# An attention-plus-gated-FFN kernel: fp32 k loads on SyncE's queue, block 1's q and k ahead of the last weights, crossbar transposes issued a phase sooner

## The chip, the cores and the metric

The kernel runs on one core of one Trainium2 chip. The metric is the device time of one execution in microseconds (us), lower is better. Profiled spans are some 2 us shorter than the times (250.0 against 251.96 us for the same execution before the change), so spans are compared with spans and times with times. TensorE is called PE in the profile, VectorE DVE, ScalarE ACT, GpSimd POOL, SyncE SP; PEld is the loading of weights into PE, which overlaps PE. "SPq" and "POOLq" are the sequencers of those engines, which issue DMAs.

## The reference, cut to what matters

q, k and v are fp32 of shape (4 batches, 8 heads, 768 positions, 64). A decayed linear attention runs over them; its output, as 3072 tokens of 512 features, goes through a gated feed-forward layer.

```
kv_state = 0
for each block of positions:
    intra = ((q k^T) * decay mask) v
    inter = (q * lam^(i+1)) kv_state
    out   = intra + inter
    kv_state = lam^block * kv_state + (k * lam^(block-1-i))^T v

y = (sigmoid(x Wg) * (x Wv)) Wo        # 512 -> 1536 -> 512
```

The kernel works in bf16 and in blocks of 128 positions, six of them (0 to 5). For one block and all four batches it needs q and k with the head dimension on the partitions, which is a transpose.

## The kernel before: the parts that the change touches

One program order is written for all engines, and each engine executes its own instructions in that order. What an engine has to wait for is decided by its own queue and by data.

The loads are GpSimd DMAs, which cast fp32 to bf16 on the way. Blocks 0 and 1 are transposed on TensorE (`t_q`, `t_k`, results tq and tk in PSUM). Blocks 2 to 5 are transposed by the DMA crossbar, issued by SyncE, from SBUF to SBUF (results qt and kt in the profile):

```
def xbar(n):                                     # blocks 2..5
    for c, d in (("q", QT), ("k", KT)):
        d[n] = qtp.tile([128, B, HP, C], BF16, tag=c + "t", name=c + "t")
        nc.sync.dma_start_transpose(out=d[n]..., in_=T_[c, n]...)

def e_q(n, bp):                                  # QS = transposed q times a table of lam powers, on VectorE
    src = tqs[n, bp] if n < FIRST_XBAR else QT[n][:, 2 * bp:2 * bp + 2]
    t = trsb.tile([128, 2, HP, C], BF16, tag="QS", name="QS")
    nc.vector.tensor_tensor(out=t, in0=src, in1=lamq..., op=ALU.mult)

def make_kd(n):                                  # kd = k times decay, on GpSimd
    nc.gpsimd.tensor_tensor(out=KD[n], in0=T_["k", n], in1=kds..., op=ALU.mult)
```

KS is the transposed k: ScalarE's copy of tk, or kt itself. The attention of a block is `piece_s` (scores sp = KS^T QS on TensorE), `piece_m` (MT = sp times mask, on VectorE), `piece_a` (op = MT v plus QS times state), `piece_x` (XT, the copy of op), and `piece_c` (state: cp on TensorE, sd on GpSimd, Sb on VectorE). The feed-forward is `piece_gv` (gp and vp, four matmuls each, 12 slices ft to a block; ScalarE makes sg, VectorE makes ht) and `piece_po` (po, 12 matmuls per batch, then an output store from SyncE). The attention of the next block is woven between the slices of the current one.

The head, before the first gp:

```
load(0, "q", 0, 2); ...; load(0, "k", 0, 2); ...; load(0, "q", 2, 4); ...; load(0, "k", 2, 4); load v; load weights
zeros(6)                       # filler matmuls, zps in the profile
t_q(0, 0); e_q(0, 0); zeros(2); t_k(0, 0); e_k(0, 0, parts=2); make_mask(); zeros(2)
piece_s(0, [0]); piece_m(0, 0); zeros(1); piece_s(0, [1]); piece_m(0, 1); zeros(2)
t_q(0, 1); e_q(0, 1); zeros(3); t_k(0, 1); e_k(0, 1, parts=2); ...; piece_s and piece_m of batches 2, 3; zeros(3)
for b in range(B): piece_a(0, [b]); piece_x(0, [b]); zeros(2 if b < B - 1 else 3)
```

And where the crossbar transposes stand:

```
for ft in range(4):  gv(1, ft, ...)
for tt in range(B):  po(0, tt, *[lambda: xbar(2)] if tt == 1 else loads if tt == 2 else [])   # behind two output stores
gv(1, 4, e_q(2)); gv(1, 5); gv(1, 6, piece_s(2), ...); ...
# later blocks: xbar(n+1) in the first slice of block n, behind the stores of block n-1
```

## Time and profile before

| | before |
|---|---|
| time, median of 4 runs | 252.57 us (252.32 to 255.6) |
| profiled span | 250.0 us |
| TensorE busy | 226.7 us (91%) |
| first gp (end of the head) | 20.47 us |
| first gp of block 1 | 50.19 us |
| first po of block 1 | 97.02 us |

The busy row of the page of the kernel before, and its row of the granted TensorE clock (tenths of full speed in 40 slices of 6.25 us):

```profile
PE 226.7 (91%) x1514; PEld 112.2 (45%) x1514; DVE 108.9 (44%) x181; ACT 76.2 (30%) x134; POOL 83.7 (33%) x73
...
PEclk9799999999996599999999999999999999999999
```

TensorE is nearly always busy, so what matters is where it is not. The list of its waits, kernel before (us in total, times, longest):

```profile
PE sp L207 <- DMA kt<-kb: 9.8, 1, 9.8
...
PE tq L166 <- DMA qb<-in_q_dram: 1.9, 1, 1.9
PE sp L207 <- DVE QS L179: 1.8, 1, 1.8
PE op L221 <- DVE MT L215: 1.2, 1, 1.2
```

One wait stands out, and it is for the transposed k of block 2. SyncE's own timeline before (start us, duration us, what) shows why it comes late:

```profile
61.40 2.92 SPq L293 DMA_DIRECT2D out_dram<-ob  x2
64.36 6.25 SPq L195 DMA_TRANSPOSE qt<-qb  x1
70.66 5.74 SPq L195 DMA_TRANSPOSE kt<-kb  x1
76.45 32.08 SPq L293 DMA_DIRECT2D out_dram<-ob  x6
```

The two transposes stand behind two output stores, and these wait for results of the po block. The records of the loads say that q of block 2 had landed at 55.4 us and k at 59.0. Each transpose keeps SyncE for about 6 us, and kt lands 12.84 us after its issue, at 83.5 us.

The wait costs more than itself. Busy time by stretch, before (stretch, length, then PE, PEld, DVE, ACT, POOL, granted clock, DMA share, GB/s), and the instructions behind the wait:

```profile
0.00:20.47 20.47, 14.93 (x127) 6.74 (x128) 9.93 (x16) 8.26 (x18) 17.14 (x24) 0.92 1.68 132
20.47:50.19 29.72, 27.19 (x225) 14.76 (x225) 18.72 (x32) 10.07 (x16) 25.80 (x24) 1.00 1.74 175
...
73.70:83.55 9.85, 0.00 (x1) 0.01 (x2) 1.89 (x3) 0.00 (x0) 6.05 (x4) 0.65 2.12 160
83.55:87.60 4.05, 4.05 (x25) 1.95 (x26) 1.29 (x2) 0.60 (x1) 1.15 (x1) 0.58 2.25 183
```

```profile
83.55 1.04 PE L207 MATMUL sp<-QS,kt 64*128 64x128 bf16 x16 [9.85 <-DMA kt<-kb]
...
84.52 1.89 PE L270 MATMUL gp<-XT,WG 128*128 128x512 bf16 x4
```

In the third stretch TensorE does nothing. In the fourth it works at a granted clock of 0.58, and the sixteen sp and four gp take 1.04 and 1.89 us instead of 0.62 and 1.03 elsewhere. The Trainium skill, "TensorE: Matmul & The Clock Gate", Part 1, says that TensorE's clock falls to half after an idle window and returns after a busy one; this trace agrees: TensorE stood idle from 73.70 us, and its clock is recorded at half from 76.73 to 86.97 us.

For the head, VectorE's timeline before:

```profile
7.44 0.69 DVE L179 TENSOR_TENSOR QS<-tq,lamq 128x1024 bf16<-128x1024 bf16 x1 [5.29 <-PE tq L166]
8.05 1.21 DVE L151 TENSOR_TENSOR mask<-tri,pk 128x1024 f32<-128x1024 f32 x1
11.34 2.48 DVE L215 TENSOR_TENSOR MT<-sp,mask 128x512 bf16<-128x512 f32 x4 [2.07 <-PE sp L207]
```

### The profile page before, as it was taken

Reading aid. Unit: us, or ns where it says so; the run is one execution under the profiler, and the core shown is the slowest. Engines: PE = TensorE matmul, PEld = TensorE weight load, DVE = VectorE, ACT = ScalarE, POOL = GpSimd, SP = SyncE. Lnnn points to the kernel's source line nnn. Section 1 sums busy time; section 2 is a strip of 40 time slices with the busy share of each in tenths; the row PEclk is TensorE's granted clock in tenths of the full one; section 3 lists DMA queues with packets and bytes.
Section 4 is the critical chain, followed back from the end, with each engine's and each line's share of the span. In section 5 each row is a group of like instructions: output and inputs, shape, how many; then the busy total and the mean of one; then the engine's idle time right before and its main releaser. Section 6 shows DMA issues by size and latency. Waiting matters only on the chain.

```text
span 250.0 us, 3742 instructions
## 1 busy us (share of the span) xinstructions
PE 226.7 (91%) x1514; PEld 112.2 (45%) x1514; DVE 108.9 (44%) x181; ACT 76.2 (30%) x134; POOL 83.7 (33%) x73
## 2 busy tenths in 40 slices
PE   4799999699970699999799999999999999999994
PEld 1344555454430345454345454455454464444443
DVE  1483657763013283048981058760087820143400
ACT  5152334221230024223224223324333252333211
POOL 8969958954993500029800023000000000000000
PEclk9799999999996599999999999999999999999999
DMA  8999999999999990275990273001290002200022
GB/s 52 150 175 184 159 161 174 206 159 152 184 166 136 198 109 3 84 166 93 156 91 3 90 173 73 4 0 42 87 210 0 3 0 85 87 0 0 0 87 84
DMA packets 104545, 24.89 MB, mean 100 GB/s; under 512 B 95696, under 2 KB 101584, under 8 KB 104528
## 3 DMA queue, kind: packets, MB, share of 16 engines
q0 software_dynamic: 84144, 14.16, 81.4%
q1 hardware_dynamic: 20384, 10.49, 17.8%
q8 instruction: 12, 0.20, 0.3%
q14 instruction: 5, 0.04, 0.1%
HBM read 28.32 MB, written 6.29 MB: 138 GB/s over the span
## 4 chain that ended last, share of the span: by engine, by line
PE 82%; DMA 8%; DVE 4%; SPq 3%; issue 1%; ACT 1%; POOL 1%; POOLq 0%; DVEq 0%
PE gp L270 24%; PE po L287 23%; PE vp L276 23%; DMA kt<-kb 5%; PE sp L207 3%; SPq L195 2%; PE op L227 2%; DMA kb<-in_k_dram 2%; PE zps L301 2%; PE cp L245 2%; DVE MT L215 2%; PE op L221 2%; DVE QS L179 2%; PE tk L173 1%; DVE ht L279 1%
## 5 line engine op out<-in xcount | busy, mean ns | idle before, releaser
L279 DVE TENSOR_TENSOR ht<-sg,vp 128x512 bf16<-128x512 bf16 x72 | 49.2, 686 | 105.4 <-PE vp L276 105.0
L270 PE MATMUL gp<-XT,WG 128*128 128x512 bf16 x288 | 74.9, 383 | 1.1 <-DVE XT L237 0.9
L276 PE MATMUL vp<-XT,WV 128*128 128x512 bf16 x288 | 74.3, 380 | 0.0
L273 ACT ACTIVATE sg<-gp 128x512 bf16<-128x512 f32 x72 | 43.0, 597 | 100.2 <-PE gp L270 99.1
L287 PE MATMUL po<-WO,ht 128*128 128x512 bf16 (+1 forms) x300 | 63.2, 371 | 0.0
L276 PEld LDWEIGHTS <-WV 128*128 128x128 bf16 x288 | 28.4, 99 | 34.5 <-issue 1.1
L287 PEld LDWEIGHTS <-ht 128*128 128x128 bf16 x300 | 29.1, 98 | 32.4
L270 PEld LDWEIGHTS <-WG 128*128 128x128 bf16 x288 | 26.9, 98 | 31.6 <-issue 1.3
L215 DVE TENSOR_TENSOR MT<-sp,mask 128x512 bf16<-128x512 f32 x48 | 30.5, 681 | 8.1 <-PE sp L207 8.1
L250 POOL TENSOR_TENSOR sd<-Sb,dec 128x512 f32<-128x512 bf16 x16 | 16.2, 1038 | 51.1 <-DVE Sb L258 51.1
L292 ACT COPY ob<-po 128x512 f32<-128x512 f32 (+1 forms) x24 | 13.8, 576 | 45.8 <-PE po L287 45.8
L93 POOL TENSOR_TENSOR kd<-kb,kds 128x2048 bf16<-128x2048 bf16 x5 | 18.2, 3639 | 0.0
L207 PE MATMUL sp<-QS,kt 64*128 64x128 bf16 x128 | 5.4, 228 | 11.7 <-DMA kt<-kb 9.8
L76 POOL DMA_DIRECT2D vb<-in_v_dram x8 | 11.4, 1425 | 7.3 <-issue 5.7
L258 DVE TENSOR_TENSOR Sb<-cp,sd 64x256 bf16<-64x256 f32 x32 | 13.5, 420 | 0.8
L239 ACT CAST XT<-op 128x512 bf16<-128x512 f32 x20 | 10.5, 598 | 10.1 <-PE op L227 10.1
L76 POOL DMA_DIRECT2D qb<-in_q_dram x8 | 11.8, 1478 | 3.9 <-issue 3.1
L301 PE MATMUL zps<-Sb 128*128 128x512 bf16 x30 | 10.5, 456 | 2.1 <-DVE Sb L110 2.1
L76 POOL DMA_DIRECT2D kb<-in_k_dram x8 | 11.5, 1433 | 1.8 <-issue 1.8
L179 DVE TENSOR_TENSOR QS<-qt,lamq 128x1024 bf16<-128x1024 bf16 x8 | 8.1, 1014 | 6.2 <-DMA qt<-qb 6.2
L207 PEld LDWEIGHTS <-kt 64*128 64x128 bf16 x128 | 3.9, 99 | 15.2 <-DMA kt<-kb 10.3
L188 ACT COPY KS<-tk 128x512 bf16<-128x512 bf16 (+1 forms) x6 | 4.2, 730 | 10.5 <-PE tk L173 10.5
(40 smaller groups left out, 84.8 us busy)
## 6 DMA issues: line engine op xcount, KB each, us to landing
out_dram<-ob SPq DMA_DIRECT2D x23, 256.0 KB, 2.0
qb<-in_q_dram POOLq DMA_DIRECT2D x4, 512.0 KB, 12.0
kb<-in_k_dram POOLq DMA_DIRECT2D x4, 512.0 KB, 15.1
vb<-in_v_dram POOLq DMA_DIRECT2D x4, 512.0 KB, 15.0
WO<-in_moe_w_out_dram POOLq DMA_DIRECT2D x3, 512.0 KB, 10.4
qb<-in_q_dram POOLq DMA_DIRECT2D x4, 256.0 KB, 7.6
kb<-in_k_dram POOLq DMA_DIRECT2D x4, 256.0 KB, 8.2
vb<-in_v_dram POOLq DMA_DIRECT2D x4, 256.0 KB, 8.4
```

The lines of the kernel that those rows point to most:

```text
L76: nc.gpsimd.dma_start(out=T_[c, n][:, b0:b1], in_=src[b0:b1, :, sl, :].rearrange("b h s d -> s (b h) d"))
L93: nc.gpsimd.tensor_tensor(out=KD[n], in0=T_["k", n], in1=kds.unsqueeze(1).unsqueeze(3).to_broadcast([128, B, H, D]), op=ALU.mult)
L207: nc.tensor.matmul(sp[u][:, hp, :], lhsT=KS[n, b][us, hp, :], rhs=QS[n, b][us, hp, :], start=(hp == 0), stop=(hp == HP - 1), skip_group_ch ...
L215: nc.vector.tensor_tensor(out=MT[n, b][:, u], in0=SP[n, b][u], in1=mask[:, u], op=ALU.mult)
L250: nc.gpsimd.tensor_tensor(out=sd, in0=Sb[:, b], in1=dec.unsqueeze(2).to_broadcast([128, HP, 128]), op=ALU.mult)
L270: nc.tensor.matmul(gp, lhsT=WG[:, mt, fs], rhs=x[:, mt, :], start=(mt == 0), stop=(mt == NMT - 1))
L273: nc.scalar.activation(sg, gp, AF.Sigmoid)
L276: nc.tensor.matmul(vp, lhsT=WV[:, mt, fs], rhs=x[:, mt, :], start=(mt == 0), stop=(mt == NMT - 1))
L279: nc.vector.tensor_mul(HT[n, ft], sg, vp)
L287: nc.tensor.matmul(po[:, :c1 - c0], lhsT=HT[n, ft][:, tt * 128:(tt + 1) * 128], rhs=WO[:, ft, c0:c1], start=(ft == 0), stop=(ft == NFT - 1))
L292: nc.scalar.copy(ob[:, c0:c1], po[:, :c1 - c0])
L301: nc.tensor.matmul(zps, lhsT=Sb[:, 0, 0, :], rhs=Sb[:, 0], start=True, stop=True)
```

## The change

Its intent has three parts (with them go smaller edits: 4 buffers instead of 5 for q and k, fewer and larger loads of block 1's v and of the output weights, and block 3's loads issued one po sooner):

- Head: k of batches 0 and 1 of block 0 comes as fp32 by SyncE's queue at once and is cast on VectorE, so half a k load leaves GpSimd's queue. The head works batch by batch, and there are fewer fillers (5 instead of 9 around op).
- Block 1: its k and q are loaded ahead of the last weight slices, and its TensorE transposes and scores are issued one slice sooner.
- Crossbar: block 2's transposes are issued ahead of the po block's stores, and those of blocks 3 to 5 late in the block before, ahead of its stores.

The diff, cut to its core:

```
+    T_["k", 0] = qkv.tile([128, B, H, D], BF16, tag="kb", name="kb", bufs=4)
+    load_hw("k", 0, nc.sync)                     # fp32 [128, H, D] by SyncE's queue
+    load_hw("k", 1, nc.sync)
+    nc.scalar.dma_start(out=lam_bc, in_=lam.partition_broadcast(128))
     load(0, "q", 0, 2)
-    nc.sync.dma_start(out=lam_bc, in_=lam.partition_broadcast(128))
...
-    load(0, "k", 0, 2)
...
     zeros(6)
-    t_q(0, 0)                                    # ... the head shown above
+    for b in range(2):
+        cast_hw("k", b)                          # VectorE, fp32 to bf16
+        t_("k", 0, [b]);  e_k(0, [b])
+        t_("q", 0, [b]);  e_q(0, [b])
+        if b == 0:
+            make_mask()
+        zeros(2)
+    for b in range(2):
+        piece_s(0, [b]);  piece_m(0, b);  zeros(1)
+    ...                                          # batches 2, 3; then op with 5 fillers
...
-    load_gv(8, 10); load q, k of block 1; load_gv(10, 11); load_gv(11, 12)
+    load k, q (batches 0, 1); load_gv(8, 9); load k, q (batches 2, 3); load_gv(9, 10); load_gv(10, 12)
...
-    behind[8] = [trans(1, 0)]                    # transposes of block 1
-    behind[9] = [pair(piece_s, 1, 0), m_(1, 0), m_(1, 1), trans(1, 1)]
-    behind[10] = [pair(piece_s, 1, 1), m_(1, 2)]
-    behind[11] = [m_(1, 3), att(1)]
+    behind[7] = [trans(1, 0)]
+    behind[8] = [pair(piece_s, 1, 0), m_(1, 0), m_(1, 1), trans(1, 1)]
+    behind[9] = [pair(piece_s, 1, 1), m_(1, 2), m_(1, 3)]
+    behind[11] = [att(1)]
...
-                gv(1, ft, *more[ft][:1] if ft < 2 else [])
+                gv(1, ft, *more[ft][:1] if ft < 2 else [lambda: xbar(2)] if ft == 3 else [])
-                po(0, tt, *[lambda: xbar(2)] if tt == 1 else loads if tt == 2 else [])
+                po(0, tt, *loads if tt == 1 else [])
-            gv(1, 10, *more[8])
+            gv(1, 10, *more[8], lambda: xbar(3))
-                more[0].append(lambda nx=nx: xbar(nx))
+                more[8].append(lambda nx=nx: xbar(nx + 1))
```

More of the change, by code (lines that the diff above doesn't have):

```diff
@@ L43 @@
     qkv = ctx.enter_context(tc.tile_pool(name="qkv", bufs=5))
+    hwp = ctx.enter_context(tc.tile_pool(name="hwp", bufs=4))
     qtp = ctx.enter_context(tc.tile_pool(name="qtp", bufs=2))
@@ L73, in load @@
             if (c, n) not in T_:
-                T_[c, n] = qkv.tile([128, B, H, D], BF16, tag=c + "b", name=c + "b")
+                T_[c, n] = qkv.tile([128, B, H, D], BF16, tag=c + "b", name=c + "b",
+                                      bufs=5 if c == "v" else 4)
             src = {"q": q, "k": k, "v": v}[c]
@@ L104, with load_hw @@
     lam_bc = const.tile([128, H], FP32, tag="lam_bc")
+    H32 = {}
+    def load_hw(c, b, eng):
+        src = {"q": q, "k": k}[c]
+        H32[c, b] = hwp.tile([128, H, D], FP32, tag="h32", name="h32")
+        eng.dma_start(out=H32[c, b], in_=src[b, :, 0:C, :].rearrange("h s d -> s h d"))
+    T_["k", 0] = qkv.tile([128, B, H, D], BF16, tag="kb", name="kb", bufs=4)
+    load_hw("k", 0, nc.sync)
+    load_hw("k", 1, nc.sync)
+    nc.scalar.dma_start(out=lam_bc, in_=lam.partition_broadcast(128))
     load(0, "q", 0, 2)
-    nc.sync.dma_start(out=lam_bc, in_=lam.partition_broadcast(128))
     nc.scalar.preload_act_table_set("natural_log_exp_and_others")
@@ L112 @@
     make_identity(nc, ident, nomemset=True)
-    load(0, "k", 0, 2)
     nc.gpsimd.iota(ip1, pattern=[[1, C]], base=1, channel_multiplier=0,
                    allow_small_or_imprecise_dtypes=True)
+    load(0, "k", 2, 4)
     for i, base in enumerate((-1, C - 1)):
@@ L118 @@
                        allow_small_or_imprecise_dtypes=True)
-    load(0, "q", 2, 4)
     nc.gpsimd.affine_select(out=tri, in_=tri, compare_op=ALU.is_gt, fill=1.0, base=0,
                             pattern=[[-1, C]], channel_multiplier=1)
-    load(0, "k", 2, 4)
+    load(0, "q", 2, 4)
     load(0, "v", 0, 2)
@@ L160, with t_, e_q, e_k @@
     tqs, tks = {}, {}
-    def t_q(n, bp):
-        tq = ps_at.tile([128, 2, HP, C], BF16, name="tq", tag="ps")
-        for i in range(2):
+    def t_(c, n, bs):
+        ps = ps_at.tile([128, len(bs), HP, C], BF16, name="t" + c, tag="ps")
+        for i, b in enumerate(bs):
             for hp in range(HP):
-                nc.tensor.transpose(tq[:, i, hp, :], T_["q", n][:, 2 * bp + i, 2 * hp:2 * hp + 2, :], ident)
-        tqs[n, bp] = tq
-    def t_k(n, bp):
-        tk = ps_at.tile([128, 2, HP, C], BF16, name="tk", tag="ps")
-        for i in range(2):
-            for hp in range(HP):
-                nc.tensor.transpose(tk[:, i, hp, :], T_["k", n][:, 2 * bp + i, 2 * hp:2 * hp + 2, :], ident)
-        tks[n, bp] = tk
-    def e_q(n, bp):
-        src = tqs[n, bp] if n < FIRST_XBAR else QT[n][:, 2 * bp:2 * bp + 2]
-        t = trsb.tile([128, 2, HP, C], BF16, tag="QS", name="QS")
-        nc.vector.tensor_tensor(out=t, in0=src,
-                                in1=lamq.unsqueeze(1).to_broadcast([128, 2, HP, C]), op=ALU.mult)
-        for i in range(2):
-            QS[n, 2 * bp + i] = t[:, i]
-    def e_k(n, bp, parts=1):
+                nc.tensor.transpose(ps[:, i, hp, :], T_[c, n][:, b, 2 * hp:2 * hp + 2, :], ident)
+        (tqs if c == "q" else tks)[n, bs[0]] = ps
+    def e_q(n, bs):
+        w = len(bs)
+        src = tqs[n, bs[0]] if n < FIRST_XBAR else QT[n][:, bs[0]:bs[0] + w]
+        t = trsb.tile([128, 2, HP, C], BF16, tag="QS", name="QS")
+        nc.vector.tensor_tensor(out=t[:, :w], in0=src,
+                                in1=lamq.unsqueeze(1).to_broadcast([128, w, HP, C]), op=ALU.mult)
+        for i in range(w):
+            QS[n, bs[i]] = t[:, i]
+    def e_k(n, bs, parts=1):
         t = trsb.tile([128, 2, HP, C], BF16, tag="KS", name="KS")
-        w = 2 // parts
+        w = len(bs) // parts
         for i in range(parts):
-            nc.scalar.copy(t[:, i * w:(i + 1) * w], tks[n, bp][:, i * w:(i + 1) * w])
-        for i in range(2):
-            KS[n, 2 * bp + i] = t[:, i]
+            nc.scalar.copy(t[:, i * w:(i + 1) * w], tks[n, bs[0]][:, i * w:(i + 1) * w])
+        for i in range(len(bs)):
+            KS[n, bs[i]] = t[:, i]
+    def cast_hw(c, b):
+        nc.vector.tensor_copy(T_[c, 0][:, b], H32[c, b])
     def xbar(n):
@@ L303 @@
     zeros(6)
-    t_q(0, 0)
-    e_q(0, 0)
-    zeros(2)
-    t_k(0, 0)
-    e_k(0, 0, parts=2)
-    make_mask()
-    zeros(2)
-    piece_s(0, [0])
-    piece_m(0, 0)
-    zeros(1)
-    piece_s(0, [1])
-    piece_m(0, 1)
-    zeros(2)
-    t_q(0, 1)
-    e_q(0, 1)
-    zeros(3)
-    t_k(0, 1)
-    e_k(0, 1, parts=2)
+    for b in range(2):
+        cast_hw("k", b)
+        t_("k", 0, [b])
+        e_k(0, [b])
+        t_("q", 0, [b])
+        e_q(0, [b])
+        if b == 0:
+            make_mask()
+        zeros(2)
+    for b in range(2):
+        piece_s(0, [b])
+        piece_m(0, b)
+        zeros(1)
+    t_("k", 0, [2, 3])
+    e_k(0, [2, 3], parts=2)
+    zeros(1)
+    t_("q", 0, [2, 3])
+    e_q(0, [2, 3])
     tables_late()
     zeros(2)
-    piece_s(0, [2])
-    piece_m(0, 2)
-    piece_s(0, [3])
-    piece_m(0, 3)
-    zeros(3)
+    for b in range(2, 4):
+        piece_s(0, [b])
+        piece_m(0, b)
     for b in range(B):
@@ L331 @@
         piece_x(0, [b])
-        zeros(2 if b < B - 1 else 3)
+        if b:
+            zeros(1)
+    zeros(2)
     make_kd(0)
     load_gv(6, 8)
-    load_gv(8, 10)
+    load(1, "k", 0, 2)
     load(1, "q", 0, 2)
-    load(1, "k", 0, 2)
+    load_gv(8, 9)
+    load(1, "k", 2, 4)
     load(1, "q", 2, 4)
-    load(1, "k", 2, 4)
-    load_gv(10, 11)
-    load_gv(11, 12)
-    load(1, "v", 0, 2)
-    load(1, "v", 2, 4)
-    for i in range(3):
-        load_wo(4 * i, 4 * i + 4)
+    load_gv(9, 10)
+    load_gv(10, 12)
+    load(1, "v")
+    load_wo(0, 6)
+    load_wo(6, 12)
     load(2, "qk")
@@ L373, in go @@
         def go():
-            t_q(n, bp)
-            e_q(n, bp)
-            t_k(n, bp)
-            e_k(n, bp)
+            bs = [2 * bp, 2 * bp + 1]
+            t_("k", n, bs)
+            e_k(n, bs)
+            t_("q", n, bs)
+            e_q(n, bs)
         return go
@@ L401 @@
             more[1] = [pair(piece_c, n, 1)]
-            more[3] = [lambda nx=nx: e_q(nx, 0)]
+            more[3] = [lambda nx=nx: e_q(nx, [0, 1])]
             more[4] = [pair(piece_s, nx, 0), m_(nx, 0)]
-            more[5] = [m_(nx, 1), lambda nx=nx: e_q(nx, 1)]
+            more[5] = [m_(nx, 1), lambda nx=nx: e_q(nx, [2, 3])]
             more[7] = [pair(piece_s, nx, 1), m_(nx, 2)]
@@ L424 @@
             if nx < NSTEP:
-                more[0].append(lambda nx=nx: xbar(nx))
                 more[2] += loads
+            if nx + 1 < NSTEP:
+                more[8].append(lambda nx=nx: xbar(nx + 1))
             for ft in range(NFT):
```

## The prediction

> What bounds the kernel now. The page's busy rows give TensorE 226.7 of 250.0 us: it is bound by TensorE plus a few waits. The list of waits on TensorE has one large entry: block 2's score matmuls wait 9.8 us for the crossbar transpose that makes kt. In the timeline, the transposes stand on SyncE behind two output stores that need results of the po block: qt is issued at 64.4 us, kt at 70.7, kt lands at 83.5, though their sources landed at 55.4 (q) and 59.0 (k). The stretch table shows a granted clock of 0.58 just after; 16 sp, 4 gp and 4 vp take 1.04, 1.82, 1.21 us there instead of 0.62, 0.97, 0.86: another 1.6 us. (The Trainium skill, "TensorE: Matmul & The Clock Gate", Part 1, says that an idle window halves the clock; this trace agrees.) So this place costs about 11.4 us. The first gp stands at 20.47 us. From there to 50.19 (first gp of block 1) TensorE is busy 27.2 of 29.7 us.
>
> What the change does.
> 1. Crossbar, block 2: the transposes stand ahead of the stores and wait only for their loads. SyncE takes 6 us to issue each and 12.8 us to land it while the software queue is full (later ones, on a quiet queue: 2 and 4.7). The loads land about 2 us sooner, because half a k load (1.8 us) left that queue: q about 53, k about 56.5. Estimate: qt issued 53, lands 66; kt issued 59, lands 72. TensorE will want kt at about 71.5. The wait shrinks from 9.8 to 0 to 2 us, and the slow clock goes: gain about 10.5 us. The skill ("DMA: Bandwidth & Descriptors", Issuing engines are not separate DMA queues) says that all queues share 16 engines, so I keep 12.8. Sooner issue for blocks 3 to 5 gains nothing: those landings (4.7 us) already precede their use; the 1.8 us wait at 124.8 is for QS on VectorE, 3.3 us long beside GpSimd's kd, and stays.
> 2. Head: k of batches 0, 1 lands by about 4.5 and 6 us instead of 8.8, but q (6.7, now sharing the engines: about 7.3) takes over. VectorE gets two casts (estimate 0.4 us each) and must do QS, mask (1.21), cast, QS before MT, so MT starts near 11.7 instead of 11.3. Fewer fillers around op (5 instead of 9) give 1 us back. First gp near 19.5: gain 1 us (0 to 2).
> 3. Block 1: transposes one slice sooner, so all MT are done before op; the waits op on MT (1.2) and tk on MT (0.3) go; the wait on XT (0.9) stays. Reordered weight slices should land some 3 us before use. Gain 1.4 us.
>
> Nothing after 130 us changes.
>
> Predicted: 252.5 - 10.5 - 1 - 1.4, about 240 us; 8 in 10 within 237 to 244.5. Chances: faster by over 2% 0.96, within 2% 0.03, slower 0.01.
>
> Signs: qt of block 2 issued near 53 us, kt landed near 72; TensorE's wait on kt under 2 us; no granted clock under 0.9 after 25 us; first gp near 19.5; first gp of block 1 near 47.7; the wait op on MT gone.
>
> What would make it wrong: transposes slowed further by the loads, kt landing at 75 us or later (each us costs one); q late in the head, or too few fillers, so that the first gp runs at half clock; a weight slice or v of block 1 late, stalling gp or op.

## The result, and the profile after

| | before | after |
|---|---|---|
| time, median | 252.57 us (4 runs, 252.32 to 255.6) | 240.02 us (4 runs, 239.52 to 241.19) |
| profiled span | 250.0 us | 237.8 us |
| head: start to first gp | 20.47 | 21.32 |
| block 0: first gp to first gp of block 1 | 29.72 | 28.35 |
| block 1: from there to its first po | 46.83 | 35.53 |
| the rest | 152.98 | 152.59 |

The ratio of the fast runs is 0.9484, 95% interval 0.9403 to 0.9565. A run counts as fast unless it is over 1.5% above the fastest of its kernel. All ratios here are the mean time of one kernel's fast runs over that of the other's fast runs of the same rounds, so they are not quite the ratio of the medians quoted.

The busy and clock rows of the page after:

```profile
PE 222.0 (93%) x1479; PEld 111.5 (47%) x1504; DVE 111.6 (47%) x184; ACT 76.5 (32%) x134; POOL 82.0 (34%) x70
...
PEclk9769999999999999999999999999999999999999
```

The dip in the 13th and 14th slice of the row (75 to 87.5 us) is gone; the early one, in the head, has grown by a slice. The waits of TensorE after:

```profile
PE tk L177 <- DVE kb L198: 2.9, 2, 1.6
PE sp L215 <- DVE QS L184: 2.2, 2, 1.8
...
PE tq L177 <- DMA qb<-in_q_dram: 1.6, 1, 1.6
```

There is no wait on kt any more, nor the 1.2 us of op on MT before block 1; that on QS in block 3 stayed. The waits in the head are on kb (the casts), which is new, and on q, which was 1.9 us before. SyncE's timeline after:

```profile
54.43 5.37 SPq L203 DMA_TRANSPOSE qt<-qb  x1
59.84 6.43 SPq L203 DMA_TRANSPOSE kt<-kb  x1
66.32 2.67 SPq L301 DMA_DIRECT2D out_dram<-ob  x4
```

The order is turned round: transposes first, issued as soon as q has landed (54.4 us) and, for kt, as SyncE is free; kt lands at 72.2 us. TensorE comes for it 0.9 us later and does not wait (timeline after, at full clock):

```profile
73.12 0.62 PE L215 MATMUL sp<-QS,kt 64*128 64x128 bf16 x16
...
73.67 1.04 PE L278 MATMUL gp<-XT,WG 128*128 128x512 bf16 x4
```

The head went the other way. VectorE's timeline after, and the chain of waits over the head (start, length, what):

```profile
8.65 0.42 DVE L184 TENSOR_TENSOR QS<-tq,lamq 128x512 bf16<-128x512 bf16 x1 [2.54 <-PE tq L177]
9.00 1.22 DVE L162 TENSOR_TENSOR mask<-tri,pk 128x1024 f32<-128x1024 f32 x1
10.13 0.53 DVE L198 CAST kb<-h 128x512 bf16<-128x512 f32 x1
...
13.18 2.48 DVE L223 TENSOR_TENSOR MT<-sp,mask 128x512 bf16<-128x512 f32 x4 [0.96 <-PE sp L215]
```

```profile
1.26 6.83 DMA qb<-in_q_dram
...
10.71 0.61 PE tk L177 x4
11.32 0.43 PE tq L177 x4
11.75 0.85 PE zps L309 x2
12.60 0.58 PE sp L215 x8
```

q lands at 8.1 us instead of 6.7, the mask and the second cast stand behind the QS that waits for it, and the matmuls of that stretch run at half clock. MT starts 1.84 us later than before. The stretch table after gives the head a granted clock of 0.84, against 0.92 before:

```profile
0.00:21.32 21.32, 13.49 (x115) 6.87 (x118) 11.50 (x19) 8.36 (x18) 17.27 (x24) 0.84 2.07 152
21.32:49.67 28.35, 26.75 (x221) 14.73 (x225) 18.72 (x32) 10.26 (x16) 26.00 (x23) 1.00 1.78 177
```

So in the spans of these two profiles: head +0.85, block 0 -1.37, block 1 -11.30, rest -0.39; together -12.2 us.

### The profile page after: what moved, and what is told of

It is laid out like the page before. It is cut to its first block, busy times and chain, and to the rows that moved or that the text cites. A ratio compares the mean times of both kernels' runs of the same rounds, so it can differ in the third digit from the quotient of the medians.

```text
span 237.8 us, 3703 instructions
## 1 busy us (share of the span) xinstructions
PE 222.0 (93%) x1479; PEld 111.5 (47%) x1504; DVE 111.6 (47%) x184; ACT 76.5 (32%) x134; POOL 82.0 (34%) x70
## 4 chain that ended last, share of the span: by engine, by line
PE 86%; DVE 8%; DMA 3%; issue 2%; DVEq 0%; POOLq 0%
PE po L295 26%; PE gp L278 25%; PE vp L284 25%; DVE MT L223 4%; DMA qb<-in_q_dram 3%; PE sp L215 3%; DVE QS L184 2%; PE op L235 2%; PE op L229 2%; PE cp L253 2%; DVE XT L245 1%; PE tq L177 1%; DVE mask L162 1%; PE tk L177 0%; PE zps L309 0%
## 5 line engine op out<-in xcount | busy, mean ns | idle before, releaser
L278 PE MATMUL gp<-XT,WG 128*128 128x512 bf16 x277 | 72.8, 379 | 1.7 <-DVE XT L245 1.1
L284 PE MATMUL vp<-XT,WV 128*128 128x512 bf16 x282 | 73.4, 379 | 0.4
L258 POOL TENSOR_TENSOR sd<-Sb,dec 128x512 f32<-128x512 bf16 x16 | 16.7, 1068 | 32.6 <-DVE Sb L266 32.6
L78 POOL DMA_DIRECT2D vb<-in_v_dram x7 | 10.8, 1541 | 8.0 <-issue 3.8
L247 ACT CAST XT<-op 128x512 bf16<-128x512 f32 x20 | 10.5, 597 | 8.0 <-PE op L235 8.0
L78 POOL DMA_DIRECT2D kb<-in_k_dram x7 | 10.3, 1469 | 7.5 <-issue 7.5
L309 PE MATMUL zps<-Sb 128*128 128x512 bf16 x18 | 7.6, 526 | 2.1 <-DVE Sb L122 2.1
L184 DVE TENSOR_TENSOR QS<-qt,lamq 128x1024 bf16<-128x1024 bf16 x8 | 9.3, 1159 | 0.0
L235 PE MATMUL op<-MT,vb 128*64 128x128 bf16 x192 | 7.3, 221 | 0.7 <-DVE MT L223 0.7
L84 POOL DMA_DIRECT2D WG<-in_moe_w_gate_dram x8 | 6.4, 794 | 1.1 <-DMA vb<-in_v_dram 1.1
```

The source lines that it names most:

```text
L78: nc.gpsimd.dma_start(out=T_[c, n][:, b0:b1], in_=src[b0:b1, :, sl, :].rearrange("b h s d -> s (b h) d"))
L184: nc.vector.tensor_tensor(out=t[:, :w], in0=src, in1=lamq.unsqueeze(1).to_broadcast([128, w, HP, C]), op=ALU.mult)
L258: nc.gpsimd.tensor_tensor(out=sd, in0=Sb[:, b], in1=dec.unsqueeze(2).to_broadcast([128, HP, 128]), op=ALU.mult)
L278: nc.tensor.matmul(gp, lhsT=WG[:, mt, fs], rhs=x[:, mt, :], start=(mt == 0), stop=(mt == NMT - 1))
L284: nc.tensor.matmul(vp, lhsT=WV[:, mt, fs], rhs=x[:, mt, :], start=(mt == 0), stop=(mt == NMT - 1))
```

## The experiments

Twelve kernels ran, each timed in 5 rounds against the kernel before. All gave correct results. The runs that put back parts of the kernel before are written in the changed kernel's functions; in the trace of x_only the 1514 matmuls and ScalarE's instructions stand in the same order as in that of the kernel before.

The table splits each profiled span at the same three marks as above; "MT" is the start of the first MT.

| run | time, median us | ratio to before | MT | head | block 0 | block 1 | rest | span |
|---|---|---|---|---|---|---|---|---|
| before | 252.57 | 1 | 11.34 | 20.47 | 29.72 | 46.83 | 152.98 | 250.00 |
| after | 240.02 | 0.9484 | 13.18 | 21.32 | 28.35 | 35.53 | 152.59 | 237.79 |
| x_only | 242.02 | 0.9608 | 11.69 | 22.23 | 29.71 | 35.31 | 152.96 | 240.21 |
| head_only | 252.54 | 1.0032 | 13.18 | 21.22 | 29.31 | 46.64 | 152.81 | 249.98 |
| b1_only | 252.49 | 1.0011 | 11.46 | 21.79 | 28.36 | 46.07 | 152.96 | 249.18 |
| old_head | 240.43 | 0.9545 | 11.42 | 21.48 | 28.36 | 35.30 | 152.97 | 238.11 |
| after_again | 240.27 | 0.9549 | 13.27 | 21.52 | 28.36 | 35.31 | 152.79 | 237.98 |
| mask_early | 240.14 | 0.9554 | 11.45 | 18.95 | 28.36 | 36.77 | 153.22 | 237.30 |
| k_by_pool | 242.33 | 0.9616 | 12.54 | 19.91 | 28.36 | 37.43 | 154.64 | 240.34 |
| hold_loads | 244.52 | 0.9697 | 13.18 | 21.36 | 28.36 | 37.50 | 155.30 | 242.52 |
| late345 | 239.97 | 0.9517 | 13.25 | 21.57 | 28.36 | 35.30 | 152.81 | 238.04 |
| eq_early | 241.94 | 0.9561 | 13.26 | 21.99 | 28.36 | 36.98 | 153.08 | 240.41 |
| mask_hold1 | 237.66 | 0.9425 | 11.45 | 19.10 | 28.36 | 35.31 | 154.49 | 237.26 |
| best | 235.22 | 0.9314 | 11.25 | 18.63 | 28.37 | 35.30 | 150.92 | 233.22 |

The time of one and the same kernel spreads by 0.7 to 3.7 us over its fast runs (head_only: 250.78 to 254.45), and the intervals of the ratios reach 0.4 to 0.8% to either side. Effects of about 1 us are therefore read in the stretches of the traces.

### The three parts alone

**x_only**: the kernel before with the crossbar moves alone.

```
-  po(0, tt, *[xbar(2)] if tt == 1 else loads if tt == 2 else [])
+  gv(1, 3, xbar(2)); po(0, tt, *loads if tt == 1 else [])       # and blocks 3..5 as in the change
```

> The kernel before with nothing changed but the place of the crossbar transposes. If the gain of block 2 is the transposes leaving the stores behind, kt lands near 73 us, TensorE's wait on kt falls from 9.8 us to 1 us or less, and the time is about 241.5 us. Rival: the gain also needs the k load off the software queue; then kt lands at 75 us or later, the wait stays at 2 us or more, and the time is 243 us or more.

kt landed at 74.6 us and TensorE, at 75.4, did not wait for it. Timeline of x_only:

```profile
61.85 6.98 SPq L200 DMA_TRANSPOSE kt<-kb  x1
...
75.39 0.62 PE L212 MATMUL sp<-QS,kt 64*128 64x128 bf16 x16
```

The time is 242.02 us, ratio 0.9608 (0.9553 to 0.9663). The place of the transposes alone takes 11.5 us out of block 1 (46.83 to 35.31), as much as in the full change; the k load off the software queue is not needed for that. Nor did block 3's loads, which this edit moves too, start sooner (56.9 us, before 55.8). The time lies 1.6 us above that of old_head (240.43), which has block 1's part besides; 1.36 us of it is block 0.

**head_only**: the kernel before with the new head.

> The kernel before with the new head alone (k of two batches as fp32 by SyncE's queue, new order of work, fewer fillers). Theory: the head costs time; first gp near 21.3 us instead of 20.5, and the time is about 253.4 us. Rival: loads that land 1 us sooner shorten the wait on kt, or the wait absorbs the late start; then the time is 252.6 us or less.

First gp at 21.22 us as expected, but the time did not move: ratio 1.0032 (0.9959 to 1.0105). Neither theory is told apart by the time. Its wait on kt was 9.78 us, as before.

**b1_only**: the kernel before with block 1's loads and transposes alone.

> The kernel before with block 1's order of loads and of transposes alone. Theory: first gp of block 1 near 48.8 us, and since the transposes of block 2 wait for the stores, they move sooner too: time about 251.2 us. Rival: kt's landing is set by traffic on the DMA engines, so the wait on kt grows by what block 1 saves: 252.5 us.

Block 0 took 28.36 us, 1.36 less than before, in this and in every other kernel with this part; the mechanism is there to the tenth. By time the run is inconclusive: 252.49 us, ratio 1.0011 (0.9953 to 1.0069). In its profile the head, which is that of before, took 21.79 instead of 20.47 us and gave block 0's gain away. The time does show it in the pair x_only and old_head, which differ by this part alone: 1.6 us.

**old_head**: the changed kernel with the head of before.

> The changed kernel with the head of before. Theory A: the head costs its 0.85 us to the end, so without it the first gp stands at 20.5 us and the time is 239.2 us. Theory B: without it q and k of block 2 land about 1 us later, kt lands near 73.2 us and TensorE, which comes 0.85 us sooner, waits about 1 us for it: the time stays at 240.0 us.

240.43 us, and no wait on kt (it landed at 72.8 us, TensorE came at 73.3). Both theories assumed a first gp at 20.5 us; it came at 21.48. So the head of before is not fixed: four profiles with it gave 20.47, 22.23, 21.79 and 21.48 us, mean 21.5. The six profiles with the new head gave 21.32, 21.22, 21.52, 21.36, 21.57 and 21.99, mean 21.5. The records of the granted clock differ in these heads: in the one of 20.47 us a single half-clock stretch of 3.4 us after the first full-clock one, in that of 22.23 us one of 6.8 us. The record starts only at its first event (14.6 us in b1_only, 14.0 us in old_head); that the clock was at half until then is read from the fillers, 0.60 to 0.63 us each there and 0.38 us later. The skill ("TensorE: Matmul & The Clock Gate", Part 1) says that the window by which the clock is set runs freely and isn't started by the kernel; these runs fit it. My reading of the two first profiles, that the head costs 0.85 us, fell: on the mean of these profiles it costs and gains nothing, though the old head's four scatter by 1.8 us, so that a few tenths can't be excluded. Inside the head two things cancel: the first MT starts 1.7 us later (mean 13.2 against 11.5), and from there to the first gp it is 1.7 us less (8.3 against 10.0).

### Where the head's gain went, and what stands behind it

**after_again**: the changed kernel once more, as a control.

> The changed kernel once more, as the control of this call: about 240.0 us, first gp near 21.3 us or within 1 us of it[...].

240.27 us, first gp at 21.52.

**mask_early**: casts and mask ahead of the first QS on VectorE.

```
     for b in range(2):
         cast_hw("k", b);  t_("k", 0, [b]);  e_k(0, [b])
+    make_mask()
+    for b in range(2):
         t_("q", 0, [b]);  e_q(0, [b])
-        if b == 0: make_mask()
         zeros(2)
```

> The changed kernel with both casts and the mask on VectorE ahead of the first q scaling, which waits for q until 8.1 us. Theory: the head is lost on VectorE's order (mask and second cast behind the late q); MT then starts near 10.2 us instead of 13.2, first gp near 18.5 instead of 21.3. kt still lands near 72.2 us, so TensorE, wanting it at 70.4, waits 1.8 us and the time is about 239.0 us. Rival: the half clock and the landing of the loads set the head; then MT starts within 1 us of before and the time is 240.0 us.

MT starts at 11.45 us, 1.8 sooner than in the control, and the first gp comes 2.6 us sooner (18.95). VectorE's order was the larger part of what the new head lost. The 0.8 us behind MT go with a half clock that ended at 12.4 us instead of 15.8. Of the expected 3.0 us for MT, 1.2 did not come; the two sets of zps and the second tq still run slowly here, which is the likely reason. The time is that of the control, 240.14 us (238.67 to 242.08). In the profile 1.9 of the 2.6 us are given back: 1.5 in block 1, 0.4 in the rest, where the wait on QS is 2.2 instead of 1.8 us. The waits of TensorE in mask_early:

```profile
PE sp L215 <- DVE QS L184: 2.2, 1, 2.2
...
PE sp L215 <- DMA kt<-kb: 1.4, 1, 1.4
```

kt lands at 72.2 us (71.9 in the control), and TensorE, which now comes at 70.8, waits 1.4 us for it. That wait is back as soon as the head is faster. It hides another: QS of block 2, 3.59 us long beside GpSimd's sd, ends at 71.7 us.

**k_by_pool**: k of batches 0 and 1 by GpSimd's queue again, no casts, the rest as changed.

```
-    load_hw("k", 0, nc.sync);  load_hw("k", 1, nc.sync)
+    load(0, "k", 0, 2)                           # GpSimd, behind q
-        cast_hw("k", b)
```

> The changed kernel with k of batches 0 and 1 loaded by GpSimd's queue with the cast in the DMA, as before the change, no casts on VectorE, all else as changed. Theory: the fp32 loads delay q from 6.7 to 8.1 us; here q lands near 6.6 and k near 8.9, MT starts near 12.3 us instead of 13.2, and loads of block 2 land about 1 us later. Time 239.5 to 240.5 us: the fp32 loads buy nothing by themselves. Rival: they buy time in the head, and the time rises to 241 us or more.

q landed at 6.1 us and k at 8.6; MT started at 12.54, 0.7 us sooner than in the control, and the first gp stood at 19.91, 1.6 us sooner. So the fp32 loads with their casts cost the head time: they delay q from 6.1 to 8.1 us. What lies behind MT, 0.9 of the 1.6 us, goes with a half clock that ended at 12.0 us instead of 15.8 and isn't shown to be theirs. (The skill, "DMA: Bandwidth & Descriptors", Issuing engines are not separate DMA queues, says that all queues run on the same 16 engines; the q load, 4.8 us without the two fp32 loads (k_by_pool) and 6.8 us beside them, agrees.) My expected time was wrong, though: 242.33 us. In block 2 VectorE's QS ran beside GpSimd's kd and sd for 4.65 us and TensorE waited 2.05 us for it, longer than kt would have held it (72.6 us landing against 71.8). In block 3, behind the wait on QS, this run had 3.4 us of half clock. So the time rises as the rival said, but not for its reason.

**hold_loads**: kd of every block ahead of the next block's loads on GpSimd.

```
-    loads = [load(nx + 1, "qkv"), make_kd(nx)]
+    loads = [make_kd(nx), load(nx + 1, "qkv")]
```

> The changed kernel with kd issued ahead of the next block's loads on GpSimd, so that block 3's loads start near 62 us instead of 54.8, after k of block 2 has landed. Theory: these loads are what slows the transposes of block 2 (12.4 us from issue to landing); kt then lands before 69 us instead of 72.2. No wait on kt is left to save, so the time stays at 240.0 us, unless kd leaves the QS that waits 1.8 us, which would give 238.5. Rival: v of block 2 alone is enough to slow them, and kt lands at 71 us or later.

The DMA list of hold_loads, over the stretch with block 2's transposes (last number: us from issue to landing):

```profile
qt<-qb SPq DMA_TRANSPOSE x1, 10.5
kt<-kb SPq DMA_TRANSPOSE x1, 9.2
```

In the control the two took 12.0 and 12.1 us. kt landed at 68.5 us: the loads of block 3 are what slows it, as the theory had it. But the time rose to 244.52 us. kd of blocks 3 and 4 now ran at the moment of a QS, which took 3.6 us (77.5) and 3.5 us (106.3) instead of 0.7; TensorE waited 2.1 and 2.6 us for them, and behind the second its clock was at half for 3.4 us. I had not expected these.

**late345**: transposes of blocks 3 to 5 back to their later place.

> The changed kernel with the transposes of blocks 3, 4 and 5 put back to their later place behind the stores; that of block 2 stays early. If their earlier issue gains nothing, as predicted, the time is 240.2 us, within 0.5 of the control, and no wait on kt shows. Rival: the earlier issue takes a wait away there; then a wait on kt or qt of 0.5 us or more shows in a later block and the time is 241 us or more.

239.97 us and no wait on kt: the earlier issue of those three blocks gains nothing, as predicted.

### VectorE's QS beside GpSimd

In the changed kernel, at the wait in block 3 (timeline after, lines of GpSimd, VectorE and TensorE):

```profile
108.46 3.65 POOL L95 TENSOR_TENSOR kd<-kb,kds 128x2048 bf16<-128x2048 bf16 x1
109.33 3.33 DVE L184 TENSOR_TENSOR QS<-qt,lamq 128x1024 bf16<-128x1024 bf16 x1
...
112.72 0.62 PE L215 MATMUL sp<-QS,kt 64*128 64x128 bf16 x16 [1.84 <-DVE QS L184]
```

QS starts 0.9 us after kd, ends 0.6 us after it, and takes 3.33 us; all QS of the same size with nothing beside them take 0.68 or 0.69. The skill, "SBUF — State Buffer", Who interferes with whom, says that VectorE and GpSimd share one pair of SBUF ports as an exclusive lock, and that a VectorE instruction with two SBUF inputs contends with a GpSimd instruction that reads SBUF; this agrees. The traces hold the counterpart: QS of block 1 has the same size but reads tq from PSUM, and wholly inside a kd it takes 0.68 us. Timeline of x_only:

```profile
43.25 3.66 POOL L94 TENSOR_TENSOR kd<-kb,kds 128x2048 bf16<-128x2048 bf16 x1
44.55 0.68 DVE L181 TENSOR_TENSOR QS<-tq,lamq 128x1024 bf16<-128x1024 bf16 x1
```

**eq_early**: the second QS of a block straight behind the first.

```
-    more[3] = [e_q(nx, [0, 1])];  more[5] = [m_(nx, 1), e_q(nx, [2, 3])]
+    more[3] = [e_q(nx, [0, 1]), e_q(nx, [2, 3])];  more[5] = [m_(nx, 1)]
```

> The changed kernel with the second q scaling of a block issued straight behind the first on VectorE, two weight slices sooner. Theory: the wait of 1.84 us on QS in block 3 comes from VectorE's QS and GpSimd's kd running at the same time, 3.3 us instead of 0.7; here QS runs while GpSimd only issues loads, takes 0.7 us, the wait is gone, and the time is 238.4 us. Rival: QS is slow for another reason (its operands, the transposes' own writes); then it stays near 3 us and the time is 240.2 us.

It failed: 241.94 us. Timeline of eq_early in block 3:

```profile
106.38 4.71 DVE L184 TENSOR_TENSOR QS<-qt,lamq 128x1024 bf16<-128x1024 bf16 x2
107.45 1.68 POOL L78 DMA_DIRECT2D kb<-in_k_dram  x1
109.11 1.71 POOL L78 DMA_DIRECT2D vb<-in_v_dram  x1
110.81 3.75 POOL L95 TENSOR_TENSOR kd<-kb,kds 128x2048 bf16<-128x2048 bf16 x1
```

Of the two QS, the first took 0.68 us and the second 4.11 (106.98 to 111.09), nearly all of it before kd started, while GpSimd issued the loads of k and v. So kd is not the only thing beside which QS is slow. That page infers that such an instruction doesn't contend with GpSimd's making of descriptors; here it ran six times as long beside it. Yet the first QS, beside the issue of q, did not, so this is an observation, and its cause was not tested further. In block 2 both QS met sd (2.81 and 1.52 us). The wait on QS turned into waits of gp on ht, 1.3 and 2.0 us, for ht stands behind QS on VectorE.

**mask_hold1**: mask_early, and kd ahead of the loads for block 2 alone.

```
-    po(0, tt, *loads if tt == 1 else [])
+    po(0, tt, *loads[::-1] if tt == 1 else [])   # kd(2), then the loads of block 3
```

> mask_early with kd of block 2 issued ahead of block 3's loads, for that block alone, so that the loads leave the transposes free. Theory: kt lands at 69 us or sooner, where TensorE wants it at 70.8; the head's 2.4 us come through, less at most 1 us where QS of block 2 meets GpSimd's sd; time 238.0 to 239.0 us, without a wait on kt. Rival: something else than the loads sets kt; a wait on kt of 1 us or more stays, 240.1 us.

kt landed at 67.4 us, no wait on it, block 1 back at 35.31 us. The time is 237.66 us, 2.3 less than that of late345, which is the changed kernel in all that matters. (Both QS of block 2 took about 0.7 us.) In its profile the rest took 1.7 us more than in the control: behind the 1.85 us wait on QS the clock was halved for a while. The stretch table of mask_hold1 around it (the clock is the third number from the end):

```profile
100.00:110.40 10.40, 8.67 (x54) 3.80 (x51) 8.90 (x11) 2.99 (x5) 9.90 (x6) 1.00 1.99 171
110.40:114.50 4.10, 3.99 (x26) 1.75 (x27) 2.82 (x6) 0.60 (x1) 0.00 (x0) 0.67 4.28 146
```

In the control the same wait had no such sequel. A wait of 1.8 us, well under the 3.4 us for which the clock is then at half, can cost twice its length, in some executions and not in others: of mask_hold1's six runs the two with a mean clock of 0.993 took 239.07 and 239.27 us, the four with 0.999 or 1.0 took 237.24 to 237.73.

**best**: mask_hold1, with block 2's QS moved into the po block and later ones straight behind each other.

```
-    po(0, tt, *loads[::-1] if tt == 1 else [])
+    po(0, tt, *loads[::-1] if tt == 1 else more[3] if tt == 2 else [])    # more[3] = both e_q(2)
-    gv(1, 4, *more[3])
+    gv(1, 4)
```

> mask_hold1 with both q scalings moved away from GpSimd's sd and kd (block 2: into the po block; later blocks: straight behind each other). If the three causes are right and independent: no wait on kt or QS after the head, first gp near 19.0 us, first gp of block 1 near 47.3, score matmuls of block 2 at 70.8, time 235.6 us. If one cause is wrong: 237 us or more.

The waits of TensorE on QS, kt and XT in best:

```profile
PE gp L278 <- DVE XT L245: 1.1, 2, 0.9
PE sp L215 <- DVE QS L184: 0.7, 1, 0.7
```

The 0.7 us is in the head; after it, only the 0.9 us for XT at the start of block 1 is left. The score matmuls of block 2 stand at 70.44 us. The time is 235.22 us (234.82 to 235.56 in 6 runs), ratio 0.9314 to before (0.9271 to 0.9356), and 4.75 us under late345. It beats both kernels. Its runs spread by 0.7 us only, but so did those of old_head (0.8), which has the wait on QS, so this doesn't show that the removed wait made it steady. After eq_early it must be said that the places of QS work here partly by chance: in block 3 both take 0.7 us, while GpSimd issues q and k.

## Why the prediction was right or wrong

The total was right, about 240 predicted and 240.02 measured, but one of its three terms was wrong, and smaller errors beside it hid that. The close agreement is luck: the terms summed to 12.9 us and the spans gave 12.2, with the head 1.85 us worse than predicted, block 1 0.8 better, 0.4 gained in the rest for which there was no term, and 239.6 rounded to 240.

**Crossbar, block 2: right, slightly under.** Predicted 10.5 us, measured 11.3 (block 1, 46.83 to 35.53), and x_only has it alone. The wait went whole and the half clock with it; the predicted remainder of 0 to 2 us was 0. qt was issued at 54.4 us (predicted 53), kt landed at 72.2 (predicted 72).

**The loads: mis-sized.** "The loads land about 2 us sooner, because half a k load left that queue." They landed 1.0 us (q, 55.4 to 54.4) and 1.1 us (k, 59.0 to 57.9) sooner. Half a k load less on that queue is worth still less: old_head and after_again, which differ by the head alone, have 0.6 us between them, and the same loads landed 1.1 us apart in before and x_only. The likely reason is that the fp32 loads took time on the same engines; it was not tested. This changed kt little: qt was issued 1.4 us later than predicted, but kept SyncE 5.4 instead of 6 us, and kt landed 12.4 instead of 12.8 us after its issue.

**Head: wrong.** "First gp near 19.5: gain 1 us." On average it is nothing (21.5 us in four old and six new heads). The step that failed is the start of MT, predicted at 11.7 us and measured at 13.2. q came at 8.1 us, not 7.3; that is 0.8 of the 1.5 us. The prediction named no clock for the matmuls between q and MT: tk, tq, zps and sp on the chain took 0.61 + 0.43 + 0.85 + 0.58 = 2.47 us at half clock, where an estimate from full-clock groups of the traces (0.22 + 0.22 + 0.43 + 0.43) is 1.3. That would more than cover the other 0.7 us, but no run separates it. The order "QS, mask, cast, QS" was seen and costed, but taken as given; mask_early shows that the order alone held 1.8 us. The 1 us that fewer fillers were to give back came, and more: from first MT to first gp is 8.14 us instead of 9.13 in these two profiles, 8.3 instead of 10.0 on the mean of all; fillers, order and clock were not separated there.

**Block 1's order: right.** Predicted 1.4 us, measured 1.37, and 1.36 in every kernel with it; the wait of op on MT before block 1 went and XT's 0.9 us stayed.

**What stays: right.** The wait of 1.8 us on QS in block 3 stayed, and blocks 3 to 5 gain nothing from the earlier transposes (late345).

**Why the total held.** The prediction had TensorE at block 2's scores at 71.5 us with kt landing at 72, nearly without slack. In fact TensorE came at 73.1, because the head gained nothing, and found kt there. Had the head gained as predicted, part of it would have been lost in the wait on kt; mask_early did just that. So the error in the head cost less than its size.

## What to carry to other kernels

A queue that executes in order is a place to look for a late start: ask for each DMA what stands ahead of it on its issuing engine, and what that waits for, before asking how fast it is. When a wait is removed, find what comes next there and by how much: here kt landed 0.9 us before its use, so the next gain in the head was lost until the loads that slow the transposes were held back. And place VectorE instructions with two SBUF inputs away from GpSimd's work, but check each place in a trace, since moving one pair away from one collision put it into another.

## What the Trainium skill lacked or had wrong

- "SBUF — State Buffer", Who interferes with whom: it infers that a VectorE instruction with two SBUF inputs isn't slowed by GpSimd's making of DMA descriptors. In eq_early such an instruction of 0.69 us took 4.11 us beside the issue of two loads, in best 1.21 and 1.52 us; beside other issues it took 0.68. What decides was not found.
- "DMA: Bandwidth & Descriptors": apart from cycle counts of earlier generations in its section on trn3, it gives no issue time for a crossbar transpose, and none under load. Here one of 512 KB keeps SyncE 5.4 to 6.4 us and lands after 12.1 to 12.8 us while the software queue is full (block 2, before and after), 2.0 to 2.5 us and 4.4 to 4.8 us on a quiet queue (blocks 3 to 5, before); holding one block's loads back brought kt's landing to 7.7 us after its issue (best).
- "TensorE: Matmul & The Clock Gate": it ties the half clock to an idle window of about 3.4 us, or to frequent short idles. In mask_hold1 a single wait of 1.85 us was followed by a granted clock of 0.67 over the next 4.1 us, while the same wait in the control was not.
